# RWKV-7 attention and a SoLU layer on one core: where the 32x32 inverse blocks are transposed

## The chip, the cores and the metric

The kernel runs on one core of one Trainium2 chip. The metric is device time in microseconds (us) for the whole program, the median of several executions; beside it there is one profiled execution, whose trace gives every number that carries a start or a duration here.

## The reference

Two blocks follow each other. The first is a delta-rule recurrence over 768 time steps, for 4 batches of 8 heads with 40 channels each; the second is a SoLU feed-forward layer (320 to 1024 to 320) on the 3072 tokens that come out.

```python
for t in range(S):                                   # S = 768, state is (B, H, 40, 40)
    y[:, :, t] = np.einsum('bhd,bhde->bhe', rt, state)
    Sa = np.einsum('bhde,bhe->bhd', state, at)
    state_decay = state * wt[:, :, None, :] - np.einsum('bhd,bhe->bhde', Sa, bt)
    state = state_decay + np.einsum('bhd,bhe->bhde', vt, kt)
...
h = x @ w_in
e = np.exp(h - np.max(h, axis=-1, keepdims=True))
sm = e / (np.sum(e, axis=-1, keepdims=True) + 1e-09)
solu = h * sm
mu = np.mean(solu, axis=-1, keepdims=True)
var = np.mean((solu - mu) ** 2, axis=-1, keepdims=True)
ln = (solu - mu) / np.sqrt(var + 1e-06) * g_ln
return (ln @ w_out).astype(np.float32)
```

## The kernel before

**Tiling.** Time is cut into 12 rounds of 64 steps (`L = 64`). A round has two steps of the program, each for two of the four batches, so the main loop runs over `i = 0 .. 23`; round `n = i // 2`. Inside a chunk the recurrence becomes a triangular system: for each of 64 pairs (batch and head, in two halves of 32 time steps) the program needs the inverse of a 32x32 unit triangular block, and then the inverse of the whole 64x64 matrix from two such blocks and the block between them.

**Parts of a step.** Each part is a Python generator that issues a few instructions at every `next`:
- `front(i)` makes the decayed keys (tile `kx`), transposes `a` and `b` on TensorE and forms the matrix `nt`. `scatter(n)` writes the diagonal blocks of `nt` to DRAM, and `gather(n)` reads them back, one block on each partition (tile `blk`).
- `invert(n)` inverts the blocks by substitution on VectorE, a row at each `next`, two instructions a row (`prod` and `u`, L492 and L494). For the rounds below `FINE = 4` it is `invert_fine`, which inverts only 16x16 blocks (L457 and L459) and leaves the last doubling to TensorE. At its end the inverse goes to DRAM twice: `u_dram`, and its transpose `ut_dram`, which VectorE or ScalarE has written to the tile `ut`.
- `bring_inverse(n)` loads both back in the layout of the products: `ti_t` (called `tinvT` in the profile) from `u_dram`, and `tn_t` (called `tinv`) from `ut_dram`.
- `attend(i)` transposes k, v and r, and makes the masked score matrices `psi` and `lamv`; the mask is a VectorE instruction (L310).
- `solve(i)` builds the 64x64 inverse: `left` multiplies with `tinv` (product `py`), `right` with `tinvT` (product `pz`), ScalarE copies both back. For fine rounds a doubling from 16 to 32 goes before it (`py16`, `y_16`, `pz16`), where `pz16` is formed twice, once for `tinvT` and once for its transpose `tinv`. Step 0 does not wait for DRAM: it doubles from 1 to 16 by itself in four levels, and keeps a transposed copy of the growing block by products of its own (`pu1`, `pu2`).
- `recurrence(i)` and `readout(i)` use the 64x64 inverse and carry the state (`sm`). `hidden(m)` and `output(m)`, with `m = i - LAG = i - 6`, are the feed-forward layer for an earlier step. `weights()` turns the layer's 64-bit weights into floats during steps 0 to 5 (tile `parts`).

**What sets the order.** The program runs under a manual schedule: each engine takes its instructions in the order in which the Python code issues them. `turns(order, ...)` reads a string; every letter advances one part. In `STEADY`, for steps 6 and on, `a` is the attention of step `i + 1`, `s` the solution of step `i + 1`, `I` a number of rows of the running inversion, `h` and `o` the layer, `B` the arrivals (`bring_inverse`, then `gather` of the next round), `X` the DMAs that repack x. How many rows an `I` gives is in `inverse_steps(i)`: from step 6 on, `[6, 7, 5]` for even and `[0, 7, 7]` for odd steps.

Around the change it is the stretch from the second `I` that matters: rows of the inversion on VectorE, then the second and the third `a` (v's transpose; the products and the mask of `psi`), then `s`, the first part of `solve`:

```python
STEADY = "r b r a r B f b b o r o I o r o y o r X I o h a f L a s a h f a I h f s h f h a f h"
```

SyncE issues nearly all DMAs, in program order, in one queue.

## Time and profile before

| what | value |
|---|---|
| median of 3 runs | 713.66 us (707.53 to 714.86) |
| profiled execution | 706.72 us, of which 705.0 us from the first to the last instruction |
| TensorE (PE) busy | 630.7 us, 89% of the span |
| VectorE (DVE) busy | 438.4 us, 62% |
| ScalarE (ACT) busy | 281.2 us, 40% |
| mean granted TensorE clock | 0.945 of full speed |
| steps 0 to 6 | 0 to 249 us |
| steps 7 to 18, two steps each | 47.5 to 48.0 us |
| last steps and the layer's rest | 535 to 705 us |

The page is read from the stage that a question belongs to: the shares above are means over stages with different limits. In rows of the timeline the columns are the start in us, the busy time in us, the engine, the line of the kernel, the operation, the tiles out<-in with their shapes, and the number of instructions merged; in square brackets stands how long the engine sat idle before it, and what ended that. PE rows give both halves of an FP32 product, so 16 products appear as x32.

## The change

Every transposed copy of an inverse block is now made by VectorE's 32x32 block transpose, from the copy that is there. `ut`, `ut_dram`, their clearing and copying and the loads of `tinv` from DRAM go; so do the products `pu1` and `pu2` of step 0 and the second half of `pz16`. The tile `tinv` has one buffer for all steps, in the layout of `tinvT`; step 0 uses its two halves for `t_0` and `y`. The tile `u` has two buffers.

There is one transpose of 128x256 per solution, before `py` (24 in all); one of 128x512 before `py16` for each fine step but step 0 (7); and four of 128x256 in step 0's doublings.

Three orders change as well. Round 0's inversion is spread among step 0's doublings, ahead of the loads for rounds 1 and 2 on SyncE's queue. The numbers of rows change for steps 0 to 6. Step 6 has a string of its own, `CENTRE`. `STEADY` is as it was, and so are the numbers of rows from step 7 on.

```diff
 def invert_fine(n):
-        for key, t, src in (("ut", ut, x.rearrange("b c t -> b t c")), ("u", u, x)):
-            dst = of_round[n][key] = dram.tile([64, Q, Q], FP32, tag=key + "_dram", name=key + "_dram")
...
+        dst = of_round[n]["u"] = dram.tile([64, Q, Q], FP32, tag="u_dram", name="u_dram")
+        for z in range(2):
+            nc.scalar.copy(out=u[half(z)][:, :, R * z:R * z + R], in_=x[half(z)])
+        for z in range(2):
+            nc.sync.dma_start(out=dst[:, R * z:R * z + R, :], in_=u[half(z)])
 def invert(n):
-        ut = two.tile([P, Q, Q // 2], FP32, tag="ut", name="ut", bufs=1)
-        nc.vector.tensor_copy(out=ut, in_=u.rearrange("p c t -> p t c"))
-        ut_dram = of_round[n]["ut"] = dram.tile([P, Q, Q // 2], FP32, tag="ut_dram", name="ut_dram")
...
-            if p == 0:
-                nc.sync.dma_start(out=ut_dram, in_=ut)
 def bring_inverse(n, steps=slice(0, 2)):
-        for q in range(4):
-            if n < FINE:
-                nc.sync.dma_start(out=tinv[quarter(q)].rearrange("s h z c -> s h (z c)"),
-                                  in_=ut[homes(q, steps)].rearrange("h s t -> s h t"))
...
 def solve(i):
         if i == 0:
...
             t = products("py1", each(level(0), eye))
-            nc.vector.tensor_tensor(out=tinv_rows, in0=unit, in1=flat(t), op=ALU.subtract)
+            nc.vector.tensor_tensor(out=t_0, in0=unit, in1=flat(t), op=ALU.subtract)
+            nc.vector.transpose(out=u_0, in_=t_0)
...
                 t = products("pz2", each(lambda q: whole(q)[2], grown))
-                nc.scalar.copy(out=tinv_rows, in_=flat(t))
-                t = products("pu2", each(grown, lambda q: whole(q)[2]))
-                nc.vector.tensor_copy(out=u_rows, in_=flat(t))
+                nc.scalar.copy(out=t_0, in_=flat(t))
+                nc.vector.transpose(out=u_0, in_=t_0)
                 yield
+        elif fine:
+            nc.vector.transpose(out=tinv, in_=tinvT)
         if fine:
             t = products("py16", [(q, whole(q)[0], whole(q)[1]) for q in range(4)])
...
-            t = products("pz16", [(q, whole(q)[3], whole(q)[2]) for q in range(4)],
-                         [(q, whole(q)[2], whole(q)[3]) for q in (0, 2)])
+            t = products("pz16", [(q, whole(q)[3], whole(q)[2]) for q in range(4)])
...
+        nc.vector.transpose(out=tinv[:, :, :, quarter(0)], in_=tinvT[:, :, :, quarter(0)])
         def left(q):
...
-    EARLY = (..., "... W I s f g W")
+    EARLY = (..., "... W I s f g W I")
+    CENTRE = "r r a r f o I r o r o y o r X I o h a f L a s a h I f s a h I f s h f s h I a f h"
 def inverse_steps(i):
         if i == 0:
-            return [4, 4, 4, 4]
+            return [4, 4, 4, 3, 1]
         if i == LAG - 1:
-            return [0, 0, 4, 5, 5]
+            return [0, 3, 4, 4, 3]
+        if i == LAG:
+            return [3, 3, 4, 4, 4]
         if i < LAG:
-            return [0, 0, 2, 3, 3] if i % 2 else [3, 3, 1, 1, 0]
+            return [0, 2, 2, 2, 2] if i % 2 else [3, 3, 1, 1, 0]
-        load(1, "v")
-        load(2, "w")
-        load(1, "r")
-        load(2, "a", "b")
-        turns("f g s f s * g a s f s * f a s g s * g W a s I f s * f a I s a g I s * g f g I W W",
-              dict(I=[2, 4, 4, 99]), f=f, g=g, s=so, a=at, I=inv, W=ws, **{"*": warmer})
-        load(2, "k")
-        scatter(1)
-        bring_inverse(0, slice(1, 2))
+        turns("f g s f s * g a s f I s * f a I s g I s * g a I", dict(I=[4, 4, 4, 99]), f=f, g=g, s=so, a=at, I=inv,
+              **{"*": warmer})
+        bring_inverse(0, slice(1, 2))
+        load(2, "w", "a", "b", "k")
+        turns("s f W s * f a s a g s g f g W W", {}, f=f, g=g, s=so, a=at, W=ws, **{"*": warmer})
+        scatter(1)
+        load(1, "v", "r")
         gather(1)
```

## What I expect

> **What bounds the kernel now.** First the page's totals and its 40 slices:

> ```profile
> span 705.0 us, 29268 instructions
> ...
> PE 630.7 (89%) x12873; PEld 448.6 (64%) x12873; DVE 438.4 (62%) x1188; ACT 281.2 (40%) x672; POOL 121.1 (17%) x226
> ...
> PEclk9869869789997999999999999999999999998999
> ...
> PE 66%; DVE 15%; ACT 6%; issue 6%; DMA 3%; SPq 2%; ACTq 0%; POOL 0%; DVEq 0%
> ```

> The third line is the granted clock, the last the chain that ended last. The dips of the clock lie in the first third, so I cut the span by stages (columns: stretch, its length, busy time of PE, PEld, DVE, ACT, POOL, then clock, DMA share, GB/s):

> ```profile
> 30.00:60.00 30.00, 21.90 (x712) 18.03 (x701) 9.31 (x30) 7.76 (x19) 5.51 (x12) 0.77 0.53 87
> 60.00:100.00 40.00, 28.94 (x638) 22.68 (x638) 25.38 (x84) 20.17 (x54) 11.33 (x22) 0.74 0.63 119
> ...
> 249.15:296.64 47.49, 46.58 (x918) 33.21 (x918) 36.32 (x97) 19.85 (x46) 8.09 (x15) 1.00 0.54 92
> ```

> There are two regimes. From step 7 to step 18 TensorE works 46.6 of 47.5 us per pair of steps at full clock: any wait put into its queue is added in full. Before that it waits, and half-clock stretches follow the waits. The steady timeline, TensorE then VectorE, of steps 8 and 9:

> ```profile
> 275.34 0.69 PE L307 MATMUL ppsi<-kx,kT 64*64 64x64 f32 x32
> 275.97 0.75 PE L567 MATMUL py<-tinv,nt 32*32 32x32 f32 x32
> ...
> 298.67 0.69 PE L307 MATMUL ppsi<-kx,kT 64*64 64x64 f32 x32
> 299.30 0.74 PE L567 MATMUL py<-tinv,nt 32*32 32x32 f32 x32
> ...
> 277.17 0.23 DVE L494 TENSOR_TENSOR u<-u,prod 128x65 f32<-128x65 f32 x1
> 277.32 0.68 DVE L310 TENSOR_TENSOR psi<-ppsi,cst 128x512 f32<-128x512 f32 x1
> 279.31 0.69 DVE L310 TENSOR_TENSOR lamv<-plamv,cst 128x512 f32<-128x512 f32 x1 [1.30 <-PE plamv L307]
> ...
> 294.97 0.48 DVE L725 TENSOR_TENSOR tot<-pyo,sm 128x320 f32<-128x320 f32 x1
> 297.45 0.56 DVE L482 TENSOR_SCALAR u<-blk 64x512 f32<-64x512 f32 x1 [2.00 <-DMA blk<-blk_dram]
> ...
> 301.86 0.68 DVE L310 TENSOR_TENSOR psi<-ppsi,cst 128x512 f32<-128x512 f32 x1
> ```

> Today py follows ppsi without a gap, since tinv came by DMA long before. VectorE is behind: it reaches psi only after its rows of the inversion, 1.35 and 2.56 us after py has started. In the changed program the transpose stands on VectorE right after psi and before lamv, and py waits for it.

> **The change, steady steps (7 to 22, solving 8 to 23).** The transpose (128x256) is in no row. The nearest, copies of 128x256 and 128x512 (L614, L498), took 0.42 and 0.61 us; I take these. Below, the 128x256 scalar operation (L178) took 0.28; above, 1.22 us as for the 128x1024 product (L785).
> Even steps: psi gives way to the next instruction 0.60 us after its start, so py starts at 277.32 + 0.60 + 0.42 + 0.05 = 278.4, not 275.97: +2.4 us. Queued behind the transpose on VectorE are lamv, the rows, kx and nmax; lamv then waited 1.30 us for plamv, which itself comes after py, so all of it slides and nothing absorbs the wait. The copy ut (0.61) that goes had 0.79 us of idle behind it (nmax waited for h) and wins nothing.
> Odd steps: by the same sum py would be late by 301.86 + 1.07 - 299.30 = 3.6. But VectorE sat idle 2.00 us for blk. The gather stood on SyncE behind three writes of u and ut and four loads of tinv; ut and these loads took 0.60 and 3.22 us of the queue in that round, so blk comes over 3 us earlier, the idle goes, and 1.6 is left.
> Sums: six even steps (8 to 18) of 2.4 make 14.4, step 20 2.3; six odd ones (7 to 17) of 1.6 make 9.6, step 19 1.5, where a later wait (1.45 us at plnT) takes a part. Steps 21 and 22 have no rows; py waits for psi and transpose alone, about 1.0 each. Together **+30 us**.

> **The clock.** Waits of TensorE have a second price. This is one, in the timeline, and then the stretch behind it (columns as above):

> ```profile
> 131.36 0.33 PE L307 MATMUL ppsi<-kx,kT 64*64 64x64 f32 x3 [2.07 <-issue]
> ```

> ```profile
> 134.00:146.50 12.50, 11.54 (x224) 9.79 (x227) 4.67 (x14) 8.61 (x24) 1.18 (x4) 0.50 0.36 86
> ```

> After 2.07 us of wait the clock is halved for over 12 us. After 2.62 us at 117.7 it stays full; after 1.45 us shortly behind 1.18 us (at 549) it is halved for some 3 us; after single waits up to 1.66 us never. So the seven even waits of 2.4 us lie where it goes either way: 0 to 3 us each, I take 1.3, together **+9**. [...]

> **Head (to 100 us).** Between the second y (28.91) and pz16 (50.17) lie 21.3 us. TensorE sat in "issue" for 2.80, 2.80 and 1.58 us there, while SyncE issued loads until 43.27; two of the three pu2 in that stretch cost some 1 us each. In the changed program the loads wait behind round 0's inversion, and VectorE's idle time (waits of 3.2 to 4.5 us) takes its rows, 0.4 to 0.5 us each, 14 of them, as well as transposes of 0.42. Adding up the new chain (y, four rows, transpose, psi, four rows, y, four rows, transpose, three rows, y_16, between them pz and py16 of about 1 us) gives some 13 us if no issue wait is left, 20 if all stay: -1 to -8, I take -7. After that TensorE waits 4.06 us at pcum for lw, which ScalarE makes only after copying round 0's inverse; the copy is now done, lw follows nt and parts at about 61.9: -2.8. The half clock after that wait (1.4 us for pcum instead of 0.7) adds -1. In step 0's remainder, blk of round 1 no longer comes 4.35 us late (its gather stood behind ut and tinv), but py16 waits for four rows and a 128x512 transpose (2.7) and py for two kx, parts, four rows and a transpose (3.4), behind which pz and pu are queued: +0.5. **Head: -10.**

> **Steps 1 to 4, fine.** On TensorE the second half of pz16 goes (0.66), on ScalarE the copies into tinv and ut (0.5 to 1.3, on the path of bT at 141.7 and 185.8: -0.9 each). Added: py16 waits for x, tot, two or three parts and the 128x512 transpose; py for kx, parts and a transpose. By the timeline: step 2, py16 127.15 to 129.7 and py 137.37 to 138.9, net +2; step 4, +2.0 and +0.8, net +1.2. Steps 1 and 3 get rows of the next inversion ahead of x, and with them a wait for blk: py16 +2.8 and +3.4, py +2.3 and +2.0, less the pz16, and 1 us of rows that no longer delays x (TensorE waits 2.62 and 1.02 us for x at 120.35 and 166.48): +3.3 and +3.7. **Together +10.**

> **Steps 5 and 6** are bound by VectorE: the chain runs through its rows from blk at 198.35 to y_16 at 227. blk comes some 2.8 us earlier, two transposes cost 1.0, and CENTRE asks for y_16 before seven rows instead of after them, which takes up to 3.9 us off the wait of 3.94 us at 227.45, against 1 for its own transposes. **-4.**

> **Sum.** 705.0 + 30 + 9 - 10 + 10 - 4 = 740 of span, 741.7 with the 1.7 us outside it. The profiled execution (706.72) lies 6.9 us under the median of the runs and just under the fastest (707.53); I add half of that, 3.5: **745 us**.

> **Rivals.**
> (a) *Every steady wait halves the clock.* For it: the 13 us after 131.36. Against: 1.66 us at 185.76 did nothing, and odd waits are that short. Fourteen waits at 3 us make 42 instead of 9: 778.
> (b) *The transpose costs more than a copy.* No row shows one. At 0.5 us more, some 24 solutions and 7 fine ones that stand on the path add 15: 760; below a copy, at 0.28, it would be 4 less. [...]
> (c) *The head wins: faster.* Stretches at half clock before 155 us add up to 48 us (twice the missing clock: 14 in 30 to 60, 21 in 60 to 100, 14 in 132 to 155), worth up to 20 us of TensorE's busy time. If the head loses its waits and they vanish, it saves 8 + 4 + 20 = 32 instead of 10; if also psi is always reached at once, as in step 21, where psi starts 0.13 us after py's old start, the steady steps cost 16 x 1.2 = 19 without a clock loss: 705.0 - 32 + 19 + 10 - 4 + 1.7 + 3.5 = 703. It decides for a gain once head and clock save more than the steady waits cost. Against it: the rows before psi are untouched, and new waits of 2.7 and 3.4 us stand in the same head.

> **How the numbers follow.** Forecast 0.52, (a) 0.18, (b) 0.10, (c) 0.20. A difference of 1% (7 us) is about what can be told from none. (c) lies across the boundary: 0.08 faster, 0.10 within 1%, 0.02 just slower; all else is slower: 0.82. The forecast's own bounds: odd steps at 3.6 add 12, the clock term at 0 takes 9, the head runs from -4 to -20, the fine steps from 0 to +13: 722 to 762. The range reaches into (c) and to most of (a): 714 to 770.

> **What would show it.** Steady pairs of steps of 51 to 53 us instead of 47.5, with a wait before py put down to a VectorE transpose of tinv, about 2.4 in even and 1.6 in odd steps; psi still behind rows; no wait for blk in odd steps; half clock after some py; lw no longer waited for at step 0; shorter issue waits before 50 us. I am wrong if steady pairs stay at 48 (VectorE is then not late, or py not held by it), or if 250 us of the old trace is reached more than 25 us sooner.

## The result, and the profile after

The changed kernel took 774.34 us (median of 4 runs, 772.23 to 778.98), the one before 713.32 on the same chip: a ratio of 1.088 (95% interval 1.080 to 1.096). The profiled execution has a span of 773.6 us against 705.0. From its page:

```profile
span 773.6 us, 28150 instructions
...
PE 643.3 (83%) x12359; PEld 456.7 (59%) x12359; DVE 446.4 (58%) x1210; ACT 273.0 (35%) x649; POOL 118.3 (15%) x218
...
PEclk9786788879888998998998998999989999998999
...
PE 54%; DVE 26%; DMA 6%; issue 5%; ACT 4%; SPq 4%; ACTq 0%; POOL 0%; DVEq 0%
```

TensorE has 514 instructions fewer and is busy 12.6 us longer; the clock row now dips all along, not only in the first third; the chain's share on VectorE went from 15% to 26%. TensorE's waits, by what it waited for (us in total, times, the longest):

```profile
PE py L547 <- DVE tinv L613: 48.1, 23, 3.7
PE py L547 <- DVE tinv L597: 41.3, 7, 11.8
```

L613 is the transpose of 128x256, L597 the one of 128x512 ahead of `py16`. Before, when `tinv` came by DMA, the products `py` waited 2.8 us in all for it. The operations are short, by the groups of VectorE (shape and count, busy time in all, mean ns):

```profile
L613 DVE STREAM_TRANSPOSE tinv<-tinvT 128x256 f32<-128x256 f32 x24 | 10.4, 434 | 0.0
L597 DVE STREAM_TRANSPOSE tinv<-tinvT 128x512 f32<-128x512 f32 x7 | 4.9, 701 | 0.0
```

So `py` waits 89.4 us in all for 15.3 us of transposing: mostly for what stands ahead of the transposes. The steady timeline of TensorE, an odd and an even step:

```profile
326.28 0.69 PE L308 MATMUL ppsi<-kx,kT 64*64 64x64 f32 x32
328.83 0.69 PE L547 MATMUL py<-tinv,nt 32*32 32x32 f32 x32 [1.85 <-DVE tinv L613]
329.45 0.66 PE L289 MATMUL prT<-cst,r 128*128 128x128 f32 x4
...
352.31 0.69 PE L308 MATMUL ppsi<-kx,kT 64*64 64x64 f32 x32
355.46 1.06 PE L547 MATMUL py<-tinv,nt 32*32 32x32 f32 x32 [2.46 <-DVE tinv L613]
356.45 1.11 PE L289 MATMUL prT<-cst,r 128*128 128x128 f32 x4
```

and the VectorE rows that the second wait stands behind:

```profile
354.13 0.23 DVE L488 TENSOR_TENSOR u<-u,prod 128x65 f32<-128x65 f32 x1
354.28 0.69 DVE L311 TENSOR_TENSOR psi<-ppsi,cst 128x512 f32<-128x512 f32 x1
354.88 0.43 DVE L613 STREAM_TRANSPOSE tinv<-tinvT 128x256 f32<-128x256 f32 x1
361.29 0.69 DVE L311 TENSOR_TENSOR lamv<-plamv,cst 128x512 f32<-128x512 f32 x1 [5.97 <-PE plamv L308]
```

Rows, `psi`, transpose, and only then `py`. After 2.46 us of wait `prT` takes 1.11 us instead of 0.66: half clock (granted 0.50 from 354.99 to 361.81). After the 1.85 us here it does not. The windows of the two steps (stretch, its length, then busy times, clock):

```profile
314.12:339.81 25.69, 23.27 (x459) 16.61 (x459) 16.94 (x47) 9.54 (x23) 3.95 (x7) 1.00 0.49 83
339.81:368.81 29.00, 26.21 (x460) 18.60 (x459) 19.59 (x52) 10.31 (x27) 3.98 (x7) 0.88 0.38 68
```

They took 23.82 and 23.67 us before. The odd step pays its wait (1.9); the even one pays its wait and 2.9 us more of TensorE's busy time.

By stages, cut at the start of `pu` of steps 0, 1, 5, 7 and 23 in the two traces:

| stage | before | after | difference | predicted |
|---|---|---|---|---|
| to `pu` of step 0 | 59.9 | 51.5 | -8.4 | |
| step 0 | 35.0 | 40.0 | +5.0 | -10 with the row above |
| steps 1 to 4 | 93.1 | 106.2 | +13.1 | +10 |
| steps 5 and 6 | 51.1 | 59.8 | +8.7 | -4 |
| steps 7 to 22 | 373.7 | 424.1 | +50.4 | +39 |
| rest | 92.3 | 92.1 | -0.2 | |

In the head the gain is there, and step 0 gives over half of it back. VectorE in step 0, and SyncE's queue before it:

```profile
70.42 0.29 DVE L447 TENSOR_SCALAR u<-blk 128x256 f32<-128x256 f32 x1 [6.68 <-DMA blk<-blk_dram]
...
72.02 0.71 DVE L597 STREAM_TRANSPOSE tinv<-tinvT 128x512 f32<-128x512 f32 x1
```

```profile
56.59 3.33 SPq L424 DMA_DIRECT2D blk_dram<-nt  x4
...
61.34 2.98 SPq L335 DMA_DIRECT2D r<-in_r_dram  x2
64.48 3.55 SPq L434 DMA_DIRECT2D blk<-blk_dram  x2
```

The first rows of round 1's inversion wait for `blk`, the transpose stands behind them, and `py16` starts only at 72.88, after 11.84 us of wait. Steps 1, 3 and 5 show the same picture with waits of 7.76, 4.11 and 8.57 us. In step 5 VectorE sat idle 5.48 us for `blk`, with x, the transpose and `py16` all behind that row:

```profile
207.04 0.42 DVE L476 TENSOR_SCALAR u<-blk 64x512 f32<-64x512 f32 x1 [5.48 <-DMA blk<-blk_dram]
...
210.04 0.68 DVE L724 TENSOR_TENSOR x<-pyo,kx 128x512 f32<-128x512 f32 x1
```

```profile
212.19 1.08 PE L547 MATMUL py<-tinv,nt 32*32 32x32 f32 x64 [8.57 <-DVE tinv L597]
```

## The experiments

My theory: the loss is the place of the transposes in VectorE's order, behind rows (which may themselves wait for a DMA), `psi` and other work; the clock adds to it. The rivals: VectorE's added work itself, and a half clock with another cause. The edits below are to the changed kernel unless said otherwise. Runs came in three groups on three chips, where the kernel before had medians of 711.96, 708.75 and 704.65; so across groups the ratios to it, and stages of the traces, are compared. Of the stages in the table, where an edit does not touch them, the stretch up to `pu` of step 0 took 49.0 to 51.8 us in the traces of the changed kernel and the runs below, step 0 36.2 to 40.0, steps 1 to 4 106.2 to 112.6, steps 5 and 6 57.0 to 59.8, and steps 7 to 22 421.1 to 424.1: smaller differences than these are not read.

**Early transpose in rounds 4 to 11.**

```diff
         nc.vector.transpose(out=tinv[:, :, :, quarter(0)], in_=tinvT[:, :, :, quarter(0)])
+        if not fine:
+            yield
-    STEADY = "... y o r X I o h a f L a s a ..."
+    STEADY = "... y o r X s I o h a f L a s a ..."
```

> Only the place changes: for rounds 4 to 11 the 128x256 transpose is issued ahead of the inversion's rows of the second I (right after x and tot), instead of behind these rows and psi. Place theory (the steady loss is py queued behind rows and psi, and the half clock that its wait brings): py waits for nothing in steps 7 to 22, the clock stays at 1.00, and a pair of steps takes 47.5 to 48 us as before the change instead of 54.7; from step 7 on the changed kernel lost 50.4 us against the one before (68.8 at pu of step 23 less 18.4 at pu of step 7), so the time falls by 45 to 50, to about 726. Rival, VectorE is the bound by its added work (0.43 us a step) wherever that stands: the wait moves to psi or kx, and the time falls by less than 10, to 765 or more.

721.27 us, ratio 1.014 (1.008 to 1.019). The same VectorE instructions in another order, and TensorE behind it (an even step):

```profile
335.67 0.48 DVE L704 TENSOR_TENSOR tot<-pyo,sm 128x320 f32<-128x320 f32 x1
336.06 0.43 DVE L613 STREAM_TRANSPOSE tinv<-tinvT 128x256 f32<-128x256 f32 x1
336.42 0.75 DVE L486 TENSOR_TENSOR prod<-blk,u 128x110 f32<-128x110 f32 x1
```

```profile
339.37 0.69 PE L308 MATMUL ppsi<-kx,kT 64*64 64x64 f32 x32
340.00 0.69 PE L547 MATMUL py<-tinv,nt 32*32 32x32 f32 x32
```

```profile
303.11:326.87 23.76, 23.19 (x459) 16.58 (x458) 17.17 (x47) 9.54 (x23) 4.10 (x7) 1.00 0.49 90
326.87:350.48 23.61, 23.28 (x459) 16.54 (x458) 19.53 (x52) 10.30 (x27) 3.97 (x7) 1.00 0.47 84
```

No wait, full clock, 47.4 us per pair; steps 7 to 22 take 371.6 us, 52.5 less than in the changed kernel and no more than before (373.7). VectorE as the bound is ruled out.

**Each early transpose twice.** `for _ in range(1 if fine else 2):` around the call, in the kernel just shown.

> As the run with early transposes in rounds 4 to 11 only, but each of these 16 transposes is made twice, one behind the other (the same values again). Theory (placed there, the transpose lies beside other work and costs nothing): within 2 us of that run, 719 to 724. Rival (VectorE has no slack, so each 0.43 us counts): 16 x 0.43 = 7 us more, 728.

722.43 us; steps 7 to 22 take 371.8 us against 371.6, where 7 us of VectorE work were added. (The ratio, 1.026, stands above the other run's 1.014; of the 1.7 us between the two traces, 719.8 against 718.1, these stages hold 0.2.) In that place 16 more transposes cost 0.2 us.

**TensorE's wait filled.** `fill` products into the unused half of the bank of `py`, the transposes where the change put them:

```diff
             t = bank(name)
+            for j in range(fill):
+                nc.tensor.matmul(t[:, 256:512], lhsT=ident, rhs=cst[:, 0:256], start=True, stop=True)
-        t = products("py", [left(0), left(2)])
+        t = products("py", [left(0), left(2)], fill=0 if fine else 4 if i % 2 else 3)
```

> TensorE's waits are filled, not shortened: 4 (even steps) or 3 (odd) products of 128x256 are issued between ppsi and py, into the unused half of py's own bank; about 0.5 us each by the 0.64 us from start to start of a 128x320 one. The transposes stay where the change put them. Clock theory (the wait itself, 2.5 us of an empty TensorE queue, takes the clock down for what follows): half-clock rows after py vanish in the steady steps, each even step loses 2.9 us (29.0 to some 26), seven of them and one odd step, so 22 us in all: about 752. Rival, half clock comes of something else in that stretch (the load on the chip, the DMAs): rows after py stay at half speed and the time stays at 774, or above it where the fillers are longer than the wait.

754.05 us, ratio 1.059 (1.054 to 1.064). The same even-step stretch:

```profile
346.50 0.69 PE L308 MATMUL ppsi<-kx,kT 64*64 64x64 f32 x32
347.12 1.99 PE L543 MATMUL py<-cst 128*128 128x256 f32 x8
349.55 0.69 PE L549 MATMUL py<-tinv,nt 32*32 32x32 f32 x32 [0.44 <-DVE tinv L615]
350.18 0.66 PE L289 MATMUL prT<-cst,r 128*128 128x128 f32 x4
```

`py` comes no sooner after `ppsi` (3.05 us; 3.15 without fillers), yet `prT` is back at 0.66. Steps 7 to 22 take 405.1 us: 19.0 of the 50.4 lost were the clock (16.0 against the shortest untouched stage, 421.1), and 31.4 the waits themselves (405.1 less 373.7). With the queue filled and the other engines' work the same (VectorE 16.93 and 19.57 us in an odd and an even step, 16.94 and 19.59 in the changed kernel), the half clock is gone (granted 1.00 from 308.40 to 360.04): it is the empty queue, not the load, that takes the clock down here.

**One filler, even steps only**: `fill=0 if fine else i % 2`.

> One product of 128x256 (some 0.5 us) is issued between ppsi and py in even steps only, so that the wait of 2.46 us before py is cut to an empty stretch of about 1.95; odd steps are as in the changed kernel. Length theory (a wait has to last some 2 us: 1.85 at 328.8 left the clock alone, 2.11 at 272.4 did not): the half clock of even steps goes, and 18 to 20 us with it: 754 to 756. Rival, it is the sum of waits, or any wait over some 1.7: half-speed rows stay, and the time is 770 to 775.

767.7 us, ratio 1.081 (1.075 to 1.087), between the two answers. The empty stretch was 1.74 us rather than 1.95. Two odd steps of this one run, both after a wait of 1.85 us:

```profile
378.76 0.69 PE L549 MATMUL py<-tinv,nt 32*32 32x32 f32 x32 [1.85 <-DVE tinv L615]
...
381.28 0.69 PE L308 MATMUL plamv<-rT,vT 64*64 64x64 f32 x32
```

```profile
430.51 0.69 PE L549 MATMUL py<-tinv,nt 32*32 32x32 f32 x32 [1.85 <-DVE tinv L615]
...
434.09 1.13 PE L308 MATMUL plamv<-rT,vT 64*64 64x64 f32 x32
```

The same wait, once with and once without half clock. Of eleven waits of 1.73 to 1.85 us in this run, seven were followed by half-speed rows; of five of 1.85 us in the changed kernel, none; of its six of 2.46 us, all. So length alone does not decide; the last section shows what goes with it.

**Old numbers of rows in steps 1, 3 and 5.**

```diff
-            return [0, 3, 4, 4, 3]
+            return [0, 0, 4, 5, 5]
-            return [0, 2, 2, 2, 2] if i % 2 else [3, 3, 1, 1, 0]
+            return [0, 0, 2, 3, 3] if i % 2 else [3, 3, 1, 1, 0]
```

> Only the numbers of rows in steps 1, 3 and 5 go back to those before the change ([0,0,2,3,3] and [0,0,4,5,5] for [0,2,2,2,2] and [0,3,4,4,3]), so that no row that waits for blk stands ahead of x, tot and the 128x512 transpose. Order theory (half of the loss up to step 7 is these rows and their wait for the DMA, with the transpose queued behind): the waits of 7.8, 4.1 and 8.6 us before py of these steps fall to 2 to 3 each, 12 us in all, some of it given back where the rows are done later: 760 to 768. Rival, the transposes themselves cost it (VectorE reaches them late by other work): waits of over 5 us stay and the time stays within 4 us of 774.

763.38 us, ratio 1.073 (1.067 to 1.078). The waits of steps 1, 3 and 5 fell from 7.76, 4.11 and 8.57 to 5.44, 1.63 and this:

```profile
201.00 0.74 PE L547 MATMUL py<-tinv,nt 32*32 32x32 f32 x64 [2.14 <-DVE tinv L597]
```

That is 11.2 us of waits less, but not 11.2 us of time. Steps 1 to 6, the stages that the edit touches, take 159.6 us, against 165.9 in the changed kernel and 166.7 to 169.6 in the four runs above, which leave them alone: 6 to 10 us. The rest of the 11 us by which the time fell lies in step 0 and in steps 7 to 22, which this edit leaves as they were; that the two figures agree is chance. Also 5.4 us in step 1 is over what I had expected, and steps 1 to 6 each kept a wait of 1.6 to 2.4 us before the second product (`py`): the rows that wait for `blk` are a part of the loss, not all.

**Gather of round 1 earlier in SyncE's queue.**

```diff
-        load(2, "w", "a", "b", "k")
+        load(2, "w", "a")
...
-        load(1, "v", "r")
         gather(1)
+        load(2, "b", "k")
+        load(1, "v", "r")
```

> Only SyncE's order in step 0 changes: the gather of round 1 goes ahead of the loads of b and k for round 2 and of v and r for round 1 (13 us of issues less ahead of it). Queue theory (py of solution 1 waits 11.8 us because VectorE's rows wait for a blk whose gather was issued at 64.5 us): blk lands near 61 us instead of 70.4, the wait of 11.8 falls to 3 to 5, and step 0 ends 7 to 9 us sooner: about 766. Rival, VectorE is late by itself (weights' parts, kx, x): the transpose stays near 72 us and the time at 774.

768.81 us, ratio 1.080 (1.075 to 1.086). The gather is issued at 55.68 instead of 64.48, and:

```profile
62.94 0.74 PE L547 MATMUL py<-tinv,nt 32*32 32x32 f32 x64 [2.53 <-DVE tinv L597]
```

Step 0 takes 30.9 us, 9.1 less, and the run 5.5 less: a part is given back. Where is not shown: step 1's wait, 9.40 us in place of 7.76, is hardly above the 7.76 to 9.27 of the traces in which nothing up to there was changed. The rival falls.

**Step 0's order as before the change.** The loads, `turns` and `bring_inverse` of the old head (the lines with a minus in the diff of the change), the transposes kept.

> The changed kernel with step 0's order as it was before the change: round 0's inversion and its stores at the end of the doublings, behind the loads of rounds 1 and 2 on SyncE; the transposes on VectorE stay. Head theory (spreading the inversion won the 8.4 us by which pu of step 0 came sooner): pu of step 0 goes back from 51.5 to 57 to 60 us, ScalarE's lw is waited for again by 3 us or more, but round 1's gather no longer has its loads ahead of it, which gives some of it back: 774 to 782. Rival, the doubling is shorter because the products pu1 and pu2 are gone: pu of step 0 stays within 2 us of 51.5, and with the earlier gather the time falls below 771.

781.62 us, ratio 1.102 (1.096 to 1.107). `pu` of step 0 is at 57.92, and the wait for `lw` is back:

```profile
62.15 1.43 PE L357 MATMUL pcum<-lw,cst 128*128 128x320 f32 x2 [3.48 <-ACT lw L353]
```

Of the 8.4 us of the head, the new order of step 0 as a whole (the spread inversion and the loads behind it) holds 6.4 in these traces. The other 2.0 (59.88 to 57.92) would be what the transposes save by themselves; that is less than the 2.8 us by which `pu` moves among runs with the same head, so it is not shown.

**Three causes undone together**: the early transpose, the old numbers of rows and the earlier gather.

> The early transpose for rounds 4 to 11, the old numbers of rows in steps 1, 3 and 5, and the gather of round 1 ahead of the loads, together; everything else as in the changed kernel. Theory (the three causes are separate: 53 + 11 + 5.5 us by their own runs): 774.3 - 69.6, about 705, which is below the kernel before (712). Rival (they cover each other, as where a shorter step 0 only lengthens the waits of step 1): over 712.

704.25 us, ratio 0.993 (0.990 to 0.996). By the ratios of the three runs (0.074, 0.016 and 0.008 less than 1.088) the sum would be 0.991, so it held, to some 2 us. By stages, 54.1 us of the gain lie in steps 7 to 22, 7.8 in step 0 and 7.1 in steps 1 to 6; the rival falls.

**The fine steps' transposes moved too**, in that kernel:

```diff
         elif fine:
             nc.vector.transpose(out=tinv, in_=tinvT)
+            yield
...
                 nc.scalar.copy(out=tinvT[rows, :, :, c:c + R], in_=t[rows, 0, :, :, R:Q])
-            yield
+            if i == 0:
+                yield
         nc.vector.transpose(out=tinv[:, :, :, quarter(0)], in_=tinvT[:, :, :, quarter(0)])
-        if not fine:
+        if i:
             yield
```

with an `s` more in the strings: "X s W a s" and "W s a I" in `EARLY`, "X s I" in `CENTRE`.

> As the one with the three causes undone, and the transposes of the fine steps moved too: the 128x512 one directly behind x and tot (ahead of parts and rows), the 128x256 one directly behind ScalarE's copies of pz16 (ahead of kx, parts and rows). Theory (the waits of 1.6 to 4 us before py16 and py in steps 2 to 6 are the same queueing): each falls by 0.5 to 2 us, 5 to 12 us in all: 693 to 700. Rival (VectorE now stands still until pz16 is copied, and kx and psi are late by as much): no faster than the kernel without these moves.

681.33 us, ratio 0.961 (0.955 to 0.968): faster than both kernels, and 22.9 us off the run before it where 5 to 12 were expected. Step 4, where the waits had been 2.13 and 1.90 us in the run before it:

```profile
154.53 0.74 PE L547 MATMUL py<-tinv,nt 32*32 32x32 f32 x64 [0.91 <-DVE tinv L597]
...
160.08 0.69 PE L547 MATMUL py<-tinv,nt 32*32 32x32 f32 x32 [0.34 <-ACT kx L372]
```

Steps 1 to 4 take 89.7 us (103.2 without these moves), steps 5 and 6 take 47.2 (55.7). Of these 22 us, TensorE's waits are 9.6, inside the 5 to 12 forecast. The other 12.3 are busy time (121.2 to 108.9 us) at a higher mean clock, 0.93 for 0.83: the forecast had left the clock out.

**The early transposes alone**, without the old numbers of rows and the earlier gather.

> The early transposes alone: those of rounds 4 to 11 as in the run of 721 us, and those of the fine steps directly behind x and tot, or behind the copies of pz16; the numbers of rows and SyncE's order in step 0 stay as the change made them. It tells how much of the loss of steps 1 to 4 belongs to the place of the transposes and how much to the rows ahead of them. Theory (the place: between the kernels with all causes undone, with and without these moves, steps 1 to 4 went from 103.2 to 89.7 us): steps 1 to 4 fall from 106 to 92 to 95 us, and the time to 700 to 706. Rival (the moves need the old numbers of rows, since x and the transpose still wait behind rows for blk): steps 1 to 4 stay over 100 us, and the time over 712.

691.96 us, ratio 0.981 (0.976 to 0.986), better than the 700 to 706 expected. Steps 1 to 4 take 95.1 us (106.2), steps 5 and 6 take 50.2 (59.8), steps 7 to 22 take 370.1. In steps 1, 3 and 5 the waits behind rows and `blk` are still there (7.93, 5.38 and 6.71 us), as the rival says; its times are not, since the other waits went. The place of the transposes by itself turns the change from 8.8% slower to 1.9% faster; rows and gather are worth another 14 us of span (690.1 to 675.7, on two chips; 2.0% by the ratios).

## Why the prediction fell short

The sign was right, and so was the mechanism of the steady steps: `py` queued behind rows and `psi` on VectorE, with half clock as a second price, and a gain in the head that does not pay for it. The time, 774, lies above the range: the span was forecast at 740 and is 773.6. Two steps hold most of the miss: steps 5 and 6 (12.7 us) and the clock (some 10).

*Steady waits, +30: right.* The run with TensorE's waits filled gives 31.4; even waits are 2.46 for 2.4, odd ones 1.85 for 1.6. The 2.00 us for which VectorE sat idle for `blk` did go.

*Clock, +9: mis-sized by 7 to 10.* I had taken 1.3 us for each of seven even waits, between 0 and 3. It was some 2.9 in each of the six even steps 8 to 18 and 1.8 in step 7, 16 to 19 in all. Six of six waits of 2.46 us in this trace halved the clock, for 6.83 us each; after the 2.07 us before 131.36 in the old trace it was down for 13.65. That it was six of six, and no odd wait after the first, of 2.11 us, has a part of luck in it, as the last section shows; so rival (a), which charged the odd waits too, is not what happened here, but in the run with one filler and in the one with the gather first some waits of 1.85 us were charged.

*Steps 5 and 6, -4: the step that failed most*, by 12.7. I priced the two transposes there at 1.0 us, their own time, and not at their place in VectorE's queue, and counted the sooner `blk` as pure gain. The new numbers of rows for step 5 put three `next`s of the inversion ahead of x, tot and the transpose; before, x (193.42) came ahead of the first row (198.35). The gather was issued 1.7 us sooner after `pu` of step 5 (4.55 us for 6.27), but VectorE now stood before `blk` with x and the transpose behind it, and `py16` waited 8.57 us. In step 6, where I had `CENTRE` gain up to 3.9 us, `py16` waited 3.86 us and `py` 2.37 behind rows, and the step grew from 29.1 to 31.2 us. The old numbers take step 5's wait to 2.14 us and the two steps to 54.7; with the transposes moved as well, they take 47.2, about the 51.1 less 4 that I had forecast.

*Head, -10: mis-sized by 6.6.* Doubling (-7) and the wait for `lw` were nearly right: -8.4 at `pu`, 0.70 us of wait for 4.06. The remainder of step 0 (+0.5) failed: py16's wait, put at 2.7 us, was 11.84 (8.9 to 11.5 in other runs with that head). I had taken away what used to hold up the gather and not counted what the new order puts there, the loads of v and r directly, and those of round 2 ahead of the scatter.

*Steps 1 to 4, +10: 3 too low* in this trace, up to 9.5 by the other runs' stages. Waits were of the right kind, step 1's (7.76) far longer than the 2.8 reckoned.

*Rival (b)*, a dear transpose, falls: 0.434 and 0.701 us against the copies' 0.42 and 0.61. *Rival (c)* falls: of the 32 us that it gave the head 3.4 came, for new waits stood there, as I had held against it, and the half clock did not go (mean clock up to `pu` of step 1: 0.80, 0.82 before).

The median lies 0.7 us over the profiled span where I had added 5.2; that took some 4 off the miss, by luck.

## What to carry to other kernels

Replacing a DMA by an operation on a busy in-order engine replaces a transfer that ran ahead by a place in a queue: cost the place, not the operation. Here 0.43 us cost 2 to 5 us behind rows and `psi`, and nothing that the stages show when issued ahead of them. And when an order changes, list for every instruction that waits on a DMA what now stands behind it.

## What had not been expected of the hardware

```profile
354.99:361.81 6.82, 6.35 (x75) 4.76 (x76) 0.85 (x2) 1.71 (x4) 0.00 (x0) 0.50 0.44 70
361.81:409.60 47.79, 43.13 (x842) 30.44 (x840) 35.59 (x98) 18.14 (x42) 7.94 (x14) 1.00 0.41 76
409.60:416.43 6.83, 6.28 (x75) 4.76 (x76) 0.86 (x3) 1.71 (x4) 0.00 (x0) 0.50 0.46 72
```

I cut the traces at times of this spacing, laid through the changes of each; 3.413 us between two of them is called a window here. Why the changes lie so is not shown. Cut by these windows, the two waits of 1.85 us shown above look different (stretch, its length, busy times of PE, PEld, DVE, ACT, POOL, then clock). The first one begins in the window before:

```profile
377.28:380.69 3.41, 1.93 (x38) 1.49 (x39) 1.30 (x4) 1.10 (x3) 0.00 (x0) 1.00 0.15 48
380.69:384.11 3.42, 3.42 (x76) 2.44 (x74) 1.90 (x6) 0.61 (x2) 0.00 (x0) 1.00 0.33 69
```

```profile
428.48:431.89 3.41, 1.55 (x50) 1.34 (x42) 1.79 (x6) 0.64 (x3) 0.00 (x0) 1.00 0.17 54
431.89:435.31 3.42, 3.42 (x39) 2.22 (x37) 0.02 (x1) 1.14 (x3) 0.00 (x0) 0.50 0.34 67
```

I took all 69 waits of 1.7 to 2.5 us before `py` in steps 7 to 20 of the five traces that have them (the changed kernel, one filler, old numbers of rows, gather earlier, old step 0), and the larger part of each that lies in one window. At up to 1.63 us none of 28 was followed by half clock, from 1.66 to 1.84 us five of 8, from 1.85 us on all 33. Length alone is not what counts: this wait of 2.46 us, in the run with the gather earlier, is cut by a window's end into some 1.75 and 0.7 us and leaves the clock alone:

```profile
293.06 0.69 PE L547 MATMUL py<-tinv,nt 32*32 32x32 f32 x32 [2.46 <-DVE tinv L613]
293.68 0.66 PE L289 MATMUL prT<-cst,r 128*128 128x128 f32 x4
```

The old trace had this already: of the 2.07 us before 131.36, which halved the clock, 1.9 lie in one window, and the 2.62 us before 120.35, which did not, are cut into 1.48 and 1.14.

The price goes with the windows too. After the 38 halving waits the clock stayed down for 3.41 us where at most 0.13 us of the wait reached into the half-clock window, and for 6.83 us where 0.17 us or more did. The second is the case of the even steps 8 to 18, with their 2.9 us; step 7 is of the first kind.

And the six even waits of the changed kernel are hardly six cases. A pair of steps takes 54.6 us there (54.76 falling to 54.62), and 16 windows are 54.61 us: every even wait falls on nearly the same place in its window, with 2.13 to 1.85 us in one, and every odd wait after the first is cut, with at most 1.28. By this sorting, another length of the pair would have given another sum. Somewhat more than half of a window, 1.85 of 3.413 us, was enough in all 33 cases. What decides between 1.66 and 1.84 us stays open.
